# Premix and postmix of talking-heads attention on the four quarters of the array, two slots at a time

## Chip, core and metric

One NeuronCore of a Trainium2 chip runs the whole kernel. Its engines work side by side, each on its own queue in order: TensorE (PE, with its weight loads PEld), VectorE (DVE), ScalarE (ACT), GpSimd (POOL) and SyncE (SP), which here only issues transfers. SBUF and PSUM have 128 partitions; PSUM has eight banks of 2 KB a partition. The metric is the device time of one execution in microseconds (us).

## What is computed

All sizes are fixed: 4 batches, 12 heads, 448 positions, head size 64.

```
scores = q @ k.T / 8                             # per head: 448 x 448
scores = einsum('bhij,hg->bgij', scores, w_pre)  # premix over the heads
e      = exp(scores - max_j);  attn = e / (sum_j e + 1e-9)
attn   = einsum('bhij,hg->bgij', attn, w_post)   # postmix over the heads
x      = attn @ v                                # 1792 tokens x 768
g      = x @ w_in;  y = (g - tanh(g)) @ w_out    # hidden 2048
# then: soft routing of the tokens to 32 slots, 8 experts, and back
```

w_in and w_out come as 64-bit floats and are converted to 32 bits by integer operations during the attention.

## The kernel before

`talking_heads` takes the queries of a batch in chunks of 120, 120, 120 and 88, sixteen in all. `scores` (L266) makes sc for two heads at a time and ScalarE copies it to S (L274), queries on the partitions. A chunk is cut into slots of at most ten queries (`attention_chunks`), 12, 12, 12 and 9 slots, 180 in all. `regroup` (L291, SyncE) moves one slot from S to a tile D with (query, head) on 120 partitions and the 448 keys along the row.

One slot then goes through these steps. `premix` (L297): pm = wpre x D, one product with a 120 x 120 weight (w_pre repeated on the diagonal, built by `kron`), 448 columns, into one PSUM bank of tag "p" (two banks); VectorE takes the negative maximum mx of each row (L299). `expo` (L306, ScalarE): e = exp(pm + mx) and the row sums ss, read by a second small instruction. `guard` (L312, GpSimd) and `recip` (L318, VectorE): rv = 1 / (ss + 1e-9). `norm` (L323, GpSimd): wk = wpost x rv. `postmix` (L333): tm = e transposed x wk, four products, each with 112 keys of e as weight columns and the 120 columns of wk moving, into one bank of tag "t" (two banks); ScalarE copies tm to aT (L336). `values` (L357) multiplies aT by v when a chunk is complete: vx, two heads at a time on the two column halves of the array.

An fp32 product appears in the trace as two records on PE and two weight loads on PEld; transposes and the products of scores (fp32r) as one.

The main loop (L514) runs over the slots s. In step s it issues the regroup of slot s + 4, planned loads, premix(s), recip and norm of s - 1, the VectorE ends of earlier jobs, postmix(s - 3), expo(s) and guard(s), then scores of the next chunk (twelve products, their four copies spread over two steps), pieces of the weight conversion (f, fa, wi, wo), and at most two jobs: k and q transposes (kx, qx; L219, L245), values. A planner spreads these over the slots. The order in which the loop issues is the order on every engine. k and v lie with four consecutive keys on one partition, 112 partitions (JP); keys appear in that permuted order everywhere.

Of the kernel before, what the change touches and what calls it, by code (L numbers as in the profile page):

```python
# [19 lines left out]
JP = SEQ // NR  # L20
# [99 lines left out]
def attention_chunks():  # L120
    out = []
    for b in range(NB):
        for i0 in range(0, SEQ, CHUNK):
            n = min(CHUNK, SEQ - i0)
            w = -(-n // IB)
            out.append((b, i0, n, [(o, len(range(o, n, w))) for o in range(w)]))
    return out


def talking_heads(tc, ident, q, k, v, w_pre, w_post, xd, box, follow):  # L130
    nc = tc.nc
    R = IB * NH
# [5 lines left out]
    DB = 5  # L138
    T_LAG = 3
# [17 lines left out]

    def load_k(b, p):
        if b:
            t = er.tile([JP, NR, 2, HD], FP32, tag="kn", name="kn", bufs=NP)  # L160
            nc.sync.dma_start(out=t, in_=k[b, 2 * p:2 * p + 2].rearrange("e (p r) d -> p r e d", r=NR))
        else:
            t = er.tile([JP, 2, NR, HD], FP32, tag="kn", name="kn", bufs=NP)
            nc.sync.dma_start(out=t, in_=k[b, 2 * p:2 * p + 2].rearrange("e (p r) d -> p e r d", r=NR))
        nat_k[b, p] = t

    def load_v(b, hf):
        t = lt.tile([JP, NP, NR, HD], FP32, tag="vn", name="vn", bufs=3)
        nc.sync.dma_start(out=t, in_=v[b, hf * NP:(hf + 1) * NP].rearrange("h (p r) d -> p h r d", r=NR))
        nat_v[b, hf] = t  # L170
# [7 lines left out]
    def kron(name, w, scale, inner_g):  # L178
        rep = lt.tile([R, NH], FP32, tag=name + "r", name=name + "r", bufs=1)
        nc.scalar.dma_start(out=rep, in_=w.unsqueeze(0).to_broadcast([IB, NH, NH]))  # L180
        m = lt.tile([R, IB, NH] if inner_g else [R, NH, IB], FP32, tag=name, name=name, bufs=1)
        if inner_g:
            src = rep.unsqueeze(1).to_broadcast([R, IB, NH])
            pat = [[-NH, IB], [0, NH]]
            neg = [[NH, IB], [0, NH]]
        else:
            src = rep.unsqueeze(2).to_broadcast([R, NH, IB])
            pat = [[0, NH], [-NH, IB]]
            neg = [[0, NH], [NH, IB]]
        nc.gpsimd.tensor_scalar(out=m, in0=src, scalar1=scale, scalar2=None, op0=ALU.mult)  # L190
        nc.gpsimd.affine_select(
            out=m, in_=m, pattern=pat, compare_op=ALU.is_ge, fill=0.0, base=0, channel_multiplier=1)
        nc.gpsimd.affine_select(
            out=m, in_=m, pattern=neg, compare_op=ALU.is_ge, fill=0.0, base=NH - 1, channel_multiplier=-1)
# [19 lines left out]
    def k_pair(b, p):  # L214
        x, read = small_bank([128, NR, JP], "kx", None if b else "x")
        src = nat_k.pop((b, p))
        for r in range(NR):
            if b:
                nc.tensor.transpose(  # L219
                    out=x[:, r, :], in_=src[:, r].rearrange("p e d -> p (e d)"), identity=ident[:JP, :JP])  # L220
            else:
                for e in range(2):
                    nc.tensor.matmul(
                        x[64 * e:64 * e + 64, r, :], lhsT=src[:, e, r, :], rhs=ident[:JP, :JP], start=True, stop=True)
        x = x.rearrange("p r j -> p (r j)")
# [68 lines left out]
    def premix(s):
        n, o, m, r = rows(s)
        x = ps.tile([R, SEQ], FP32, tag="p", name="pm")
        nc.tensor.matmul(x[:r], lhsT=wpre[:r, :m, :], rhs=D_t.pop(s)[:r], start=True, stop=True)  # L297
        mx = lt.tile([R, 1], FP32, tag="mx", name="mx", bufs=3)
        nc.vector.tensor_reduce(out=mx[:r], in_=x[:r], op=ALU.max, axis=AX.X, negate=True)  # L299
        pp_t[s], mx_t[s] = x, mx  # L300

    def expo(s):
        n, o, m, r = rows(s)
        e = lt.tile([R, SEQ], FP32, tag="e", name="e", bufs=T_LAG + 1)
        ss = lt.tile([R, 1], FP32, tag="ss", name="ss", bufs=3)
        nc.scalar.activation(out=e[:r], in_=pp_t.pop(s)[:r], func=ACTF.Exp, bias=mx_t.pop(s)[:r], accum_out=ss[:r])  # L306
        e_t[s], ss_t[s] = e, ss

    def guard(s):
        n, o, m, r = rows(s)  # L310
        rv = lt.tile([R, 1], FP32, tag="rv", name="rv", bufs=3)
        nc.gpsimd.tensor_scalar(out=rv[:r], in0=ss_t.pop(s)[:r], scalar1=EPS, scalar2=None, op0=ALU.add)  # L312
        ss_t[s] = rv

    def recip(s):
        n, o, m, r = rows(s)
        rv = ss_t[s]
        nc.vector.reciprocal(out=rv[:r], in_=rv[:r])  # L318

    def norm(s):  # L320
        n, o, m, r = rows(s)
        wk = lt.tile([R, NH, IB], FP32, tag="wk", name="wk", bufs=T_LAG)
        nc.gpsimd.tensor_scalar(out=wk[:r], in0=wpost[:r], scalar1=ss_t.pop(s)[:r], scalar2=None, op0=ALU.mult)  # L323
        wk_t[s] = wk

    def postmix(s):
        n, o, m, r = rows(s)
        if o == 0:
            attn_t[n] = lt.tile([JP, NR, NH, CHUNK], FP32, tag="aT", name="aT", bufs=2)
        e, wk = e_t.pop(s), wk_t.pop(s)  # L330
        x = ps.tile([JP, NR, NH, IB], FP32, tag="t", name="tm", bufs=2)
# [1080 lines left out]
```

## Time and profile before

| | |
|---|---|
| median of 3 executions | 929.73 us (928.1 to 933.96) |
| profiled execution, span from first to last instruction | 926.1 us |
| TensorE busy | 894.8 us, 97% |
| VectorE, ScalarE, GpSimd busy | 564.2, 573.3, 295.6 us |
| DMA moved | 223.95 MB, 242 GB/s |
| chain of waits | PE 90%, DMA 4%, ACT 2%, DVE 2% |

The profile shows one execution. Busy time is the time in which an engine has at least one instruction running; matmuls overlap and their ends are modelled. The chain of waits follows the work that ended last back to the start, at each step to what released it. The shares of the whole span mix the attention with the products behind it, so the views that matter are those by stretches. The span is the profiled execution's own time as far as the profile shows it; the executions that were timed include what lies around it.

### The profile page before, as it was taken

The page shows a single profiled execution, that of the slowest core. Times are in us where ns is not written, and L with a number is a line of the kernel's source. Part 1 is how long each engine was busy: PE and PEld are TensorE (multiplying, and loading weights), DVE is VectorE, ACT ScalarE, POOL GpSimd, SP SyncE. Part 2 cuts the span into 40 slices and gives each one's busy share as a digit, 9 for nine tenths or more (in the row PEclk, how much of TensorE's full clock was granted, in tenths as well). Part 3 has the DMA queues.
Part 4 walks back from the last instruction along what each step waited for, and adds up shares of the span by engine and source line. Part 5 has one row for each costly group of instructions (what it writes and reads, how often), then busy time and mean ns, then how long its engine had stood idle before and what let it go on. Part 6 is the DMA issues. An engine that isn't in the chain of part 4 may idle for free.

```text
span 926.1 us, 19424 instructions
## 1 busy us (share of the span) xinstructions
PE 894.8 (97%) x6926; PEld 658.9 (71%) x6926; DVE 564.2 (61%) x1267; ACT 573.3 (62%) x1299; POOL 295.6 (32%) x499
## 2 busy tenths in 40 slices
PE   8989999999999999999999999999999998999995
PEld 6667777777777777777778677767776776875453
DVE  3566757767678676686555576566866677740103
ACT  4766767777777777777665667546664666730013
POOL 1464445644446544565431223000000014610000
PEclk9999999999999999999999999999999999998998
DMA  6988688866889766684457878669754536879998
GB/s 138 236 215 230 202 235 221 246 208 198 228 226 245 224 184 212 201 249 166 145 213 260 309 248 274 241 247 361 309 207 168 171 106 219 306 292 424 424 375 310
DMA packets 145780, 223.95 MB, mean 242 GB/s; under 512 B 60756, under 2 KB 127380, under 8 KB 142100
## 3 DMA queue, kind: packets, MB, share of 16 engines
q1 hardware_dynamic: 142336, 209.83, 70.6%
q10 hardware_dynamic: 3348, 12.87, 3.6%
q8 instruction: 56, 0.92, 0.4%
q14 instruction: 40, 0.33, 0.1%
HBM read 147.96 MB, written 36.18 MB: 199 GB/s over the span
## 4 chain that ended last, share of the span: by engine, by line
PE 90%; DMA 4%; ACT 2%; DVE 2%; issue 1%; POOL 0%; ACTq 0%; POOLq 0%; SPq 0%; DVEq 0%
PE hp L755 24%; PE pm L297 15%; PE tm L333 14%; PE vx L357 9%; PE sc L266 7%; DMA D<-S 3%; PE h L1197 3%; PE gt L826 3%; PE so L1238 2%; PE tz L1217 2%; PE lgp L876 2%; PE sp L958 1%; PE wt L845 1%; PE qx L245 1%; PE op L1294 1%
## 5 line engine op out<-in xcount | busy, mean ns | idle before, releaser
L333 PEld LDWEIGHTS tm<-wk,e 120*112 120x112 f32 (+1 forms) x1440 | 174.0, 177 | 70.6 <-issue 58.5
L299 DVE TENSOR_REDUCE mx<-pm 120x1 f32<-120x448 f32 x180 | 111.9, 622 | 126.0 <-PE pm L297 125.4
L336 ACT ACTIVATE aT<-tm 112x480 f32<-112x480 f32 x180 | 105.4, 585 | 120.1 <-PE tm L333 120.1
L297 PE MATMUL pm<-D,wpre 120*120 120x448 f32 x360 | 174.1, 566 | 5.2 <-DMA D<-S 4.7
L333 PE MATMUL tm<-wk,e 120*112 120x120 f32 (+1 forms) x1440 | 176.7, 266 | 1.0 <-POOL wk L323 1.0
L323 POOL TENSOR_SCALAR wk<-wpost,rv 120x120 f32<-120x120 f32 x180 | 124.8, 693 | 137.4 <-PE tm L333 116.0
L755 PE MATMUL hp<-xa,rg 128*128 128x512 f32 x576 | 152.5, 405 | 0.0
L755 PEld LDWEIGHTS hp<-xa,rg 128*128 128x128 f32 x576 | 102.5, 189 | 28.5 <-issue 10.7
L306 ACT ACTIVATE e<-pm,mx 120x448 f32<-120x448 f32 x180 | 113.4, 630 | 4.9 <-DVE rv L318 2.4
L717 POOL TENSOR_TENSOR rg<-rg 128x384 fp32r<-128x384 f32 x32 | 31.9, 1011 | 206.3 <-DVE rg L714 191.4
L274 ACT ACTIVATE S<-sc 120x448 f32<-120x448 f32 (+1 forms) x186 | 90.6, 543 | 7.3 <-PE sc L266 3.0
L357 PE MATMUL vx<-aT,vn 112*64 112x120 f32 (+1 forms) x1536 | 84.0, 263 | 0.0
L786 DVE SCALAR_TENSOR_TENSOR qd<-qd,sq 128x512 f32<-128x512 f32 (+1 forms) x62 | 38.3, 617 | 69.9 <-ACT mk L782 63.5
L357 PEld LDWEIGHTS vx<-aT,vn 112*64 112x64 f32 x1536 | 73.9, 137 | 6.1 <-issue 0.9
L775 ACT ACTIVATE sq<-hp 128x512 f32<-128x512 f32 (+1 forms) x62 | 32.8, 530 | 71.7 <-PE hp L755 71.7
L755 PE MATMUL hp<-xb,rg 128*128 128x512 f32 x288 | 74.8, 405 | 0.0
L312 POOL TENSOR_SCALAR rv<-ss 120x1 f32<-120x1 f32 x180 | 42.7, 237 | 97.0 <-ACT e L306 83.6
L297 PEld LDWEIGHTS pm<-D,wpre 120*120 120x120 f32 x360 | 51.4, 182 | 27.7 <-ACT e L306 10.7
L266 PE MATMUL sc<-khi,qT 64*120 64x448 f32 (+1 forms) x384 | 68.8, 387 | 0.8 <-DVE qT L249 0.8
L68 POOL TENSOR_TENSOR fa<-fa,f 128x384 f32<-128x384 f32 x64 | 65.2, 1019 | 5.3 <-issue 0.2
L755 PEld LDWEIGHTS hp<-xb,rg 128*128 128x128 f32 x288 | 52.0, 188 | 16.6 <-issue 6.3
L708 POOL TENSOR_TENSOR rg<-rg 128x768 fp32r<-128x768 f32 x13 | 24.0, 1845 | 67.8 <-PE gt L826 33.5
(177 smaller groups left out, 1351.6 us busy)
## 6 DMA issues: line engine op xcount, KB each, us to landing
ex<-in_moe_w_dram SPq DMA_DIRECT2D x25, 1536.0 KB
D<-S SPq DMA_DIRECT2D x172, 210.0 KB
rg<-wis SPq DMA_DIRECT2D x32, 768.0 KB
f<-in_moe_w_in_dram SPq DMA_DIRECT2D x32, 384.0 KB
f<-in_moe_w_out_dram SPq DMA_DIRECT2D x32, 384.0 KB
wis<-rg ACTq DMA_DIRECT2D x16, 768.0 KB
rg<-wi SPq DMA_DIRECT2D x26, 384.0 KB
wi<-fa SPq DMA_DIRECT2D x32, 192.0 KB
```

Source lines behind the costliest of these rows:

```text
L68: eng.tensor_tensor(out=out, in0=bits(a), in1=bits(p), op=ALU.add)
L266: nc.tensor.matmul(xs[e][0][:ni], lhsT=qT[n][s, l, p, :ni], rhs=kt[s], start=(i == 0), stop=(i == 2))
L274: nc.scalar.activation(out=dst, in_=xs[e][0][:ni], func=ACTF.Copy)
L297: nc.tensor.matmul(x[:r], lhsT=wpre[:r, :m, :], rhs=D_t.pop(s)[:r], start=True, stop=True)
L299: nc.vector.tensor_reduce(out=mx[:r], in_=x[:r], op=ALU.max, axis=AX.X, negate=True)
L306: nc.scalar.activation(out=e[:r], in_=pp_t.pop(s)[:r], func=ACTF.Exp, bias=mx_t.pop(s)[:r], accum_out=ss[:r])
L312: nc.gpsimd.tensor_scalar(out=rv[:r], in0=ss_t.pop(s)[:r], scalar1=EPS, scalar2=None, op0=ALU.add)
L323: nc.gpsimd.tensor_scalar(out=wk[:r], in0=wpost[:r], scalar1=ss_t.pop(s)[:r], scalar2=None, op0=ALU.mult)
L333: nc.tensor.matmul(x[:, c, :, :m], lhsT=e[:r, c * JP:(c + 1) * JP], rhs=wk[:r, :, :m], start=True, stop=True)
L336: nc.scalar.activation(out=attn_t[n][:, :, :, c0:c0 + m], in_=x[:, :, :, :m], func=ACTF.Copy)
L357: nc.tensor.matmul(x[64 * e:64 * e + 64, i, :ni], lhsT=nat_v[b, h // NP][:, h % NP, c, :], rhs=a[:, c, h, :ni], start=(c == 0), stop=(c == ...
L755: nc.tensor.matmul(hp, lhsT=r32(w[:, m, hl, cs]), rhs=r32(x_of(b, c, l)), start=(c == 0 and i == 0), stop=(c == KD - 1 and i == 2))
```

## The change

A slot's ten queries are split: queries 0 to 4 lie on partitions 4 to 63, queries 5 to 9 on 64 to 123, four zero rows ahead. The mixing of the heads never crosses queries, so the weight falls into two blocks of 64 x 64. Two slots (a pair) go together. Premix is four products of 64 x 64 with 448 columns: the row half is the half x of the queries, the column half is the slot i; the result xs[x] has the first slot on partitions 0 to 63 and the second on 64 to 127. Postmix is 32 products: for each x and each run c of 128 keys, slot i on row half i, key half z on column half z, 64 key columns of weight and 60 moving. To make this fit, keys lie on 128 partitions, four to a partition on the first 64 and three on the others, so k and v come in two transfers each. The slot count of a chunk is now even: 12, 12, 12, 10, 184 in all, 92 pairs. A pair takes both banks of "p" and, for postmix, both of "t". The copy to aT is a step of its own (`gather`), one loop step behind postmix; where a slot has fewer than ten queries it takes two instructions.

```diff
-    DB = 5
-    T_LAG = 3
+    DB = 6
+    T_LAG = 4
...
-            w = -(-n // IB)
+            w = 2 * -(-n // (2 * IB))
...
+    def load_rows(t, src):
+        nc.sync.dma_start(out=t[:64], in_=src[:, :JL].rearrange("h (p r) d -> p h r d", r=NR))
+        nc.sync.dma_start(out=t[64:, :, :NR - 1], in_=src[:, JL:].rearrange("h (p r) d -> p h r d", r=NR - 1))
...
     def regroup(s):
-        t = lt.tile([R, SEQ], FP32, tag="D", name="D", bufs=DB)
+        t = ds[s % DB]
-        nc.sync.dma_start(out=t[:r], in_=S_t[n][o:ni:w])
+        nc.sync.dma_start(out=t[4:4 + m * NH], in_=S_t[n][o:ni:w])
...
     def premix(s):
-        x = ps.tile([R, SEQ], FP32, tag="p", name="pm")
-        nc.tensor.matmul(x[:r], lhsT=wpre[:r, :m, :], rhs=D_t.pop(s)[:r], start=True, stop=True)
+        xs = [ps.tile([128, SEQ], FP32, tag="p", name="pm") for _ in range(2)]
+        d = [D_t.pop(s + i) for i in range(2)]
+        for x, k0, k1 in ((0, 0, 64), (1, 64, 64 + (m - IH) * NH)):
+            for i in range(2):
+                nc.tensor.matmul(
+                    xs[x][64 * i:64 * i + 64], lhsT=wpre[k0:k1], rhs=d[i][k0:k1], start=True, stop=True)
...
+            nc.vector.tensor_reduce(out=mx[:, x:x + 1], in_=xs[x], op=ALU.max, axis=AX.X, negate=True)
...
     def expo(s):
+            nc.scalar.activation(
+                out=es[x], in_=xs[x], func=ACTF.Exp, bias=mx[:, x:x + 1], accum_out=ss[:, x:x + 1])
...
     def norm(s):
+            wk = lt.tile([128, NH, IH], FP32, tag="wk", name="wk", bufs=2 * EB)
+            nc.gpsimd.tensor_scalar(out=wk, in0=wpost, scalar1=rv[:, x:x + 1], scalar2=None, op0=ALU.mult)
...
     def postmix(s):
-        for c in range(NR):
-            nc.tensor.matmul(
-                x[:, c, :, :m], lhsT=e[:r, c * JP:(c + 1) * JP], rhs=wk[:r, :, :m], start=True, stop=True)
+        xs = [ps.tile([128, 2, NR, NH, IH], FP32, tag="t", name="tm", bufs=2) for _ in range(2)]
+        for x in range(2):
+            for c in range(NR):
+                for i in range(2):
+                    for z in range(2):
+                        h = slice(64 * i, 64 * i + 64)
+                        j = min(128 * c + 64 * z, SEQ - 64)
+                        nc.tensor.matmul(
+                            xs[i][64 * z:64 * z + 64, x, c], lhsT=es[x][h, j:j + 64], rhs=wks[x][h],
+                            start=True, stop=True)
...
+        if s % 2 == 0:
+            if live:
+                premix(s)
+            for f in late:
+                f()
+            if 0 <= s - T_LAG < NS:
+                postmix(s - T_LAG)
+            if live:
+                expo(s)
+                guard(s)
+        else:
+            if s - 1 < NS:
+                recip(s - 1)
+                norm(s - 1)
+            for f in late:
+                f()
+            if 0 <= s - 1 - T_LAG < NS:
+                gather(s - 1 - T_LAG)
```

TensorE's queue in the middle of the attention, before (the number behind a name is the buffer; "x4" are four products in a row):

```order
L297 MATMUL pm_3951<-D_3794,wpre_134 120x448
L333 MATMUL tm_3960<-wk_3877,e_3839 112x120 x4
L297 MATMUL pm_3978<-D_3824,wpre_134 120x448
L333 MATMUL tm_3985<-wk_3909,e_3885 112x120 x4
L266 MATMUL sc_3997<-khi_2819,qT_3605 120x448
```

The same place after the change; the tm rows go on in this way, sixteen of them:

```order
L321 MATMUL pm_5043<-D_135,wpre_151 64x448
L321 MATMUL pm_5043<-D_136,wpre_151 64x448
L321 MATMUL pm_5044<-D_135,wpre_151 64x448
L321 MATMUL pm_5044<-D_136,wpre_151 64x448
L364 MATMUL tm_5052<-wk_4920,e_4898 64x60 x2
L364 MATMUL tm_5053<-wk_4920,e_4898 64x60 x2
L364 MATMUL tm_5052<-wk_4920,e_4898 64x60 x2
L364 MATMUL tm_5053<-wk_4920,e_4898 64x60 x2
```

Two slots' premix and postmix, which alternated, stand as one block of four and one of 32 products, and other products come only behind the block.

ScalarE's queue in the middle of the attention, before:

```order
L336 ACTIVATE aT_3779<-tm_3912 112x48x10
L306 ACTIVATE e_3918,ss_3919<-pm_3904,mx_3906 120x448
L47 ACTIVATE fa_3924<-f64_3681 128x384
L336 ACTIVATE aT_3779<-tm_3960 112x48x10
L306 ACTIVATE e_3966,ss_3967<-pm_3951,mx_3953 120x448
```

The same after:

```order
L333 ACTIVATE e_4898,ss_4900<-pm_4855,mx_4861 128x448
L333 ACTIVATE e_4899,ss_4900<-pm_4856,mx_4861 128x448
L295 ACTIVATE S_4461<-sc_4841 120x448
L295 ACTIVATE S_4461<-sc_4842 120x448
L267 ACTIVATE qT_4545<-qx_4911 128x360
L378 ACTIVATE aT_4830<-tm_4864 128x48x10
L378 ACTIVATE aT_4830<-tm_4865 128x48x10
L48 ACTIVATE fa_4927<-f64_4642 128x384
```

The copies of tm stood ahead of the e of the same step; they now stand behind the pair's two e and whatever the even step holds.

## Rows read from the trace of the kernel before

**Rows 1.** The page: span, busy time of the engines.

```profile
span 926.1 us, 19424 instructions
...
PE 894.8 (97%) x6926; PEld 658.9 (71%) x6926; DVE 564.2 (61%) x1267; ACT 573.3 (62%) x1299; POOL 295.6 (32%) x499
```

**Rows 2.** Busy time by stretches; columns in the first row.

```profile
core 0: us, PE busy (x) PEld busy (x) DVE busy (x) ACT busy (x) POOL busy (x), PEclk, DMA share, GB/s
...
22.00:60.00 38.00, 33.05 (x204) 22.99 (x205) 21.69 (x54) 28.75 (x74) 19.24 (x45) 1.00 0.90 228
...
150.00:200.00 50.00, 50.00 (x441) 38.19 (x440) 36.97 (x98) 38.01 (x95) 28.37 (x50) 1.00 0.90 249
...
250.00:300.00 50.00, 50.00 (x439) 38.19 (x438) 37.58 (x97) 37.54 (x93) 28.20 (x49) 1.00 0.91 239
```

**Rows 3.** The same view, 75 to 489 us.

```profile
75.00:489.00 414.00, 412.12 (x3623) 316.33 (x3623) 282.78 (x711) 300.35 (x741) 208.10 (x376) 1.00 0.73 213
```

**Rows 4.** The chain of waits, 75 to 489 us, shares by line.

```profile
by line: PE pm L297 32.1%; PE tm L333 31.3%; PE vx L357 17.7%; PE sc L266 12.9%; PE kx L219 1.7%; PE qx L245 1.7%; DMA D<-S 1.3%; PE hp L755 1.1%; issue 0.4%; DVE xa L741 0.3%; ACT e L306 0.2%; DVE mx L299 0.1%; POOL wk L323 0.1%; ACT S L27
```

**Rows 5.** The same stretch, premix's line alone (L297).

```profile
75.00:489.00 414.00, 151.89 (x314) 44.84 (x314) 1.00 0.73 213
```

**Rows 6.** The chain in order of time, 22 to 80 us: start, length, what.

```profile
37.50 10.50 DMA D<-S
...
66.69 1.79 PE vx L357 x32
...
69.72 5.53 DMA D<-S
```

**Rows 7.** TensorE in order of time (start, length, line, operation), plain slots, then scores.

```profile
254.94 1.01 PE L297 MATMUL pm<-D,wpre 120*120 120x448 f32 x2
255.79 0.98 PE L333 MATMUL tm<-wk,e 120*112 120x120 f32 x8
256.61 0.92 PE L297 MATMUL pm<-D,wpre 120*120 120x448 f32 x2
...
258.54 0.37 PE L266 MATMUL sc<-klo,qT 64*120 64x448 f32 x2
258.74 0.57 PE L266 MATMUL sc<-khi,qT 64*120 64x448 f32 x4
```

**Rows 8.** The same, windows 854.985 to 855.013 and 855.44 to 855.48 us: four strips.

```profile
854.99 0.13 PEld L1197 LDWEIGHTS h<-ex,siT 128*32 128x32 f32 x4
854.99 0.64 PE L1197 MATMUL h<-ex,siT 128*32 128x512 f32 x4
...
854.99 1.07 PE L1197 MATMUL h<-ex,siT 128*32 128x512 f32 x8
```

**Rows 9.** Weight loads of vx, windows 302.00 to 302.02 and 302.05 to 302.07 us.

```profile
302.00 0.14 PEld L357 LDWEIGHTS vx<-aT,vn 112*64 112x64 f32 x2
...
302.00 0.20 PEld L357 LDWEIGHTS vx<-aT,vn 112*64 112x64 f32 x4
```

**Rows 10.** Weight loads of 128 columns, 521 us.

```profile
520.99 0.97 PEld L865 LDWEIGHTS wq<-seld,ex 96*128 96x128 f32 x8 [0.25 <-ACT ex L860]
```

**Rows 11.** The page's groups: busy, mean ns, idle time before.

```profile
L299 DVE TENSOR_REDUCE mx<-pm 120x1 f32<-120x448 f32 x180 | 111.9, 622 | 126.0 <-PE pm L297 125.4
...
L323 POOL TENSOR_SCALAR wk<-wpost,rv 120x120 f32<-120x120 f32 x180 | 124.8, 693 | 137.4 <-PE tm L333 116.0
```

**Rows 12.** ScalarE in order of time, 307 to 310 us.

```profile
307.24 0.59 ACT L336 ACTIVATE aT<-tm 112x480 f32<-112x480 f32 x1 [0.39 <-PE tm L333]
307.71 0.62 ACT L306 ACTIVATE e<-pm,mx 120x448 f32<-120x448 f32 x1
...
308.31 0.96 ACT L274 ACTIVATE S<-sc 88x448 f32<-88x448 f32 x2
309.16 0.55 ACT L47 ACTIVATE fa<-f 128x384 f32<-128x384 f32 x1
```

**Rows 13.** SyncE's issues at the start.

```profile
18.82 6.02 SPq L291 DMA_DIRECT2D D<-S  x7
```

More of the change, by code (lines that the diff above doesn't have):

```diff
@@ new lines, in kron @@
+        if pre:
+            m = lt.tile([128, 64], FP32, tag=name, name=name, bufs=1)
+            nc.gpsimd.memset(m, 0.0)
+            for x in range(2):
+                nc.gpsimd.tensor_copy(
+                    out=m[64 * x:64 * x + 64, 4:], in_=big[64 * x:64 * x + 64, IH * x:IH * x + IH].rearrange("p i g -> p (i g)"))
+        else:
+            m = lt.tile([128, NH, IH], FP32, tag=name, name=name, bufs=1)
+            for x in range(2):
+                nc.gpsimd.tensor_copy(out=m[64 * x:64 * x + 64], in_=big[64 * x:64 * x + 64, x])
@@ L296, in premix @@
[L296 to L307 removed]
+        m = rows(s)[2]
@@ L309, in guard @@
+        pp_t[s], mx_t[s] = xs, mx
+    def expo(s):
+        es = [lt.tile([128, SEQ], FP32, tag="e", name="e", bufs=2 * EB) for _ in range(2)]
+        ss = lt.tile([128, 2], FP32, tag="ss", name="ss", bufs=2)
+        xs, mx = pp_t.pop(s), mx_t.pop(s)
+        for x in range(2):
+            nc.scalar.activation(
+                out=es[x], in_=xs[x], func=ACTF.Exp, bias=mx[:, x:x + 1], accum_out=ss[:, x:x + 1])
+        e_t[s], ss_t[s] = es, ss
     def guard(s):
-        n, o, m, r = rows(s)
@@ L311, in guard @@
[L311 to L312 removed]
+        rv = lt.tile([128, 2], FP32, tag="rv", name="rv", bufs=2)
+        nc.gpsimd.tensor_scalar(out=rv, in0=ss_t.pop(s), scalar1=EPS, scalar2=None, op0=ALU.add)
         ss_t[s] = rv
     def recip(s):
[L316 to L318 removed]
+        nc.vector.reciprocal(out=ss_t[s], in_=ss_t[s])
@@ L320, in norm @@
     def norm(s):
[L321 to L324, printed above, removed]
-    def postmix(s):
[L327 to L331, printed above, removed]
-        for c in range(NR):
-            nc.tensor.matmul(
-                x[:, c, :, :m], lhsT=e[:r, c * JP:(c + 1) * JP], rhs=wk[:r, :, :m], start=True, stop=True)
-        c0 = sum(z for q, z in chunks[n][3] if q < o)
-        nc.scalar.activation(out=attn_t[n][:, :, :, c0:c0 + m], in_=x[:, :, :, :m], func=ACTF.Copy)
+        rv = ss_t.pop(s)
@@ new lines, in gather @@
+    def gather(s):
+        for i, x in enumerate(tm_t.pop(s)):
+            n, o, m = rows(s + i)
+            if o == 0:
+                attn_t[n] = lt.tile([128, NR, NH, CHUNK], FP32, tag="aT", name="aT", bufs=2)
+            c0 = sum(z for q, z in chunks[n][3] if q < o)
+            out = attn_t[n].rearrange("p r h i -> p (r h) i")
+            x = x.rearrange("p x r h i -> p (r h) x i")
+            if m == 2 * IH:
+                nc.scalar.activation(
+                    out=out[:, :, c0:c0 + m].rearrange("p a (x i) -> p a x i", x=2), in_=x, func=ACTF.Copy)
+            else:
+                nc.scalar.activation(out=out[:, :, c0:c0 + IH], in_=x[:, :, 0], func=ACTF.Copy)
+                nc.scalar.activation(out=out[:, :, c0 + IH:c0 + m], in_=x[:, :, 1, :m - IH], func=ACTF.Copy)
@@ L513, in talking_heads @@
     s = 0
-    while s < NS + T_LAG + 2 or jobs or late:
+    while s < NS + T_LAG + 3 or jobs or late:
         live = s < NS
```

96 lines of the change are left out of this document (53 added, 43 removed).

## Prediction

> **What bounds the kernel now.** I read the page first, then a table by stretches, then the chain of waits of the long stretch, then single instructions. The profiled execution has a span of 926.1 us [rows 1]; the three times shown have a median of 929.73 us, 3.6 us more, and the sum below is made against 926.1. TensorE is busy 97% of the span, but that is an average over two halves. The slot loop runs from 22 to 489 us; everything behind it is untouched by the change.
>
> From 75 to 489 us TensorE is busy 412.12 of 414 us; ScalarE 300.35, VectorE 282.78, GpSimd 208.10, the DMA engines 0.73 [rows 3]. The chain of waits there is pm 32.1%, tm 31.3%, vx 17.7%, sc 12.9%: TensorE waits for nothing [rows 4]. pm has 314 records, two to an fp32 product, so this is 157 slots, 78.5 pairs of 5.27 us [rows 5].
>
> From 22 to 75 us it is another story. TensorE is busy 33.05 of 38 us (87%) while the DMA engines are at 0.90 [rows 2], and the chain holds transfers D<-S, of 10.50 and 5.53 us among them [rows 6]: premix waits for its rows. A faster premix gains nothing there.
>
> **The change, part by part.**
>
> *Premix.* A plain slot shows what it costs: pm starts at 254.94, tm at 255.79, the next pm at 256.61 [rows 7]. The last gap, 0.82 us, is tm's; the pm behind it (0.92 us with its drain) costs 0.75 until tm may follow, so pm + tm are 1.57 us a slot and 3.14 us a pair. After, a pair has four 64x64 products of the same 448 columns, eight records on four quarters. If the quarters run together, that is two rounds of 0.375 us, 0.75, and I put 0.05 for the first weights: 0.80 us a pair in place of 1.50. The trace has no 64x64 product. It has the two halves of the idea apart. Halves of the rows: sc, 448 columns in one pass (0.19 us, half of a pm record's two passes), comes in pairs 0.20 us apart, at 258.54 and 258.74 [rows 7]. Parts of the columns: four h records on four strips take 0.64 us together and eight take 1.07 [rows 8], so a further round of four costs 0.43 us, the streaming time of one (512 columns where pm's 448 take 0.375). Bounds: 0.75 when both compose, 1.50 when only one does.
>
> *Postmix.* Before, 16 records a pair of 120 columns, 0.82 us a slot [rows 7]. After, 32 products, 64 records of 64 weight columns and 60 moving columns, 16 rounds on four quarters. Two things can set a round. The moving part is half of tm's 0.10 us: 0.05 us. The weight load: two vx loads of 64 columns, one on each column half, end together after 0.14 us, four after 0.20 [rows 9], so a second load on the same half costs 0.06 us; eight of 128 columns take 0.97 us [rows 10], 0.12 each, 0.06 for 64. Loads of the two halves run together. So a round is 0.06 us, bound by the loads, and a pair costs 16 x 0.06 = 0.96, with the first load 0.98 us in place of 1.64. Bounds: 0.82 (the moving part alone) and 64 x 0.055 = 3.5 us (every load by itself). I take 0.98, since it is the load that the vx rows show on halves.
>
> How fast records can follow one another matters at 64 a pair. In a window of 0.028 us four loads and four products of h have all begun [rows 8], so records of different strips go out some 0.007 us apart with their loads. A round of four has 0.06 us to go out in. [...]
>
> *TensorE's sum.* 5.27 - 3.34 us (pm and tm by their 63.4% of the chain) leaves 1.93 us a pair for vx, sc, kx, qx; none of these changes its columns. The queries of the 88-row chunks now make 10 slots in place of 9, so 184 slots, 161 of them behind the first 23: 80.5 pairs. TensorE then needs 0.80 + 0.98 + 1.88 = 3.66 us a pair, 295 us.
>
> *What is late next.* With TensorE that short, the others have no slack. ScalarE: 300.35 us / 80.5 = 3.73 us a pair; the 88-row chunks' slots copy aT in two pieces (40 slots; a second piece between nothing and 0.55 us, the fa row of 384 elements [rows 12]; I take 0.2), 0.1 more. VectorE 3.5. The DMA engines 0.73 x 414 / 80.5 = 3.75 us. All lie between 3.5 and 3.85, so the loop no longer has one bound but four.
>
> The pair also loses double buffering: pm's two banks and tm's two banks now both belong to one pair. So the next postmix waits for both aT copies, and these stand behind two e on ScalarE, which wait for mx, which waits for pm. Followed round for two pairs: tm 0.98, other products 1.88, pm 0.80 and its drain 0.17, the first mx 0.62 [rows 11] with 0.1 of handing over, two e at 0.60 (307.71 to 308.31 [rows 12]), on average one S copy 0.43 and 0.3 of fa and qT, two aT at 0.47: 7.4 us, 3.7 a pair. Queued behind the waiting e are the S copies that free the banks of sc; behind the waiting tm stand sc and vx.
>
> Four demands of 3.5 to 3.85 us that must meet in one order will not fill each other's gaps. The one stretch where TensorE shares the bound is 22 to 60 us: 87% busy. 3.66 / 0.87 = 4.2 us a pair. Bounds: 3.7 (no friction) and 4.7 (as much friction again).
>
> *DMA.* Bytes and rows stay; k and v tiles come as two transfers instead of one, 32 more issues on SyncE, 0.86 us each by the D<-S rows (seven in 6.02 us [rows 13]): 28 us over the loop, before which SyncE's 180 D<-S issues are 155 us of 467; it has room. In 150 to 200 and 250 to 300 us the DMA share is 0.90 and 0.91 already [rows 2]: these cannot go below 45 us each, while 4.2/5.27 would make them 40. I add 2 x 5 us.
>
> *At the start.* The six first kn loads become twelve. At the 0.86 us of an issue that is up to 5 us if all of it is on the path, nothing if the warm-up products cover it; I take 2. The new GpSimd setup (zero rows, larger masks) lies ahead of the first pm at 21.9 us, on an engine that is nearly idle until then. Its 22 operations at wk's 0.69 us [rows 11] would be 15 us; what went over 21.9 would cost its full length.
>
> *GpSimd and VectorE in the loop.* rv and its reciprocal halve in number, wk stays two a pair at half the columns: nothing on the path, since GpSimd has 208 of 414 us.
>
> **Sum.** 22 to 75 us: unchanged. 75 to 489: 80.5 x 4.2 = 338, and 10 for the DMA: 348 in place of 414, -66. Start +2. 926.1 - 64 = 862, and 3.6 outside the span: **866 us**.
>
> **Rivals.**
> 1. *TensorE stays the only bound.* ScalarE and DMA times are unions that include waits and contention, and shrink when pressed. Then 3.66 us a pair, 295, and 10 for the DMA: -109 + 2, **823 us**. For it: two demands of 0.73 left TensorE no gap at all before. Against: single banks, and the 87% of 22 to 60 us. 0.10.
> 2. *Postmix gains little: records go out too slowly, or two quarters run at a time.* tm stays at 1.6 to 1.86 us a pair (32 rounds of 0.058), TensorE needs 4.28 to 4.54; it is then the longest demand again, and half the friction (a factor of 1.075) makes 4.6 to 4.9 us a pair, 370 to 394, with no DMA addition: **888 to 912 us**. If premix runs in twos as well (pm 1.5), TensorE needs 5.24 us, 422: **940 us** at most, about no change. For it: no row has 64 records in a microsecond. Against: the h rows. 0.14, and 0.06 for about no change. [...]
> 3. *The other side: weight loads of the quarters go one after another.* tm 64 x 0.055 = 3.5 us, 0.80 + 3.5 + 1.88 = 6.2 us a pair on TensorE alone; over 92 pairs 570 us in place of 467: **1,035 us**. The change turns into a loss when a pair exceeds 414 / 80.5 = 5.14 us; without friction that is tm at 2.46 us, 38 ns a record, with half of it 2.1 us, 33 ns. vx, with two halves, makes a record per 56 ns (32 in 1.79 us [rows 6]). Against: vx is bound by its 120 columns, not by loads, and its loads overlap. 0.11.
>
> **How the numbers follow.** The likeliest, 0.59: 866, its own range 840 to 895 (3.9 to 4.55 us a pair). Rival 1 0.10, rival 2 0.14, about no change 0.06, rival 3 0.11. The range 820 to 920 leaves out some 0.03 below and 0.17 above. A measurement of this kernel can tell about 1%, 9 us, from no change: faster 0.83, same 0.06, slower 0.11.
>
> **What would show it.** tm: 64 records in about 1.0 us, rounds 0.06 us apart; pm: the pair's four products within 0.8 us and a drain. In 75 to 475 us TensorE below 90% busy, ScalarE and DMA each near 0.9. Chain: pm and tm together under 45%, with ACT e, ACT aT or DMA D<-S in it. TensorE at 97% with a shorter loop would be rival 1; tm records 25 ns or more apart rival 2; 50 ns rival 3. [...]

## Result and the profile after

| | before | after |
|---|---|---|
| median of the executions run together | 928.99 us (4) | 918.12 us (4; 913.11 to 922.78) |
| ratio to before, 95% interval | | 0.9874, 0.9825 to 0.9923 |
| profiled execution, span | 926.1 us | 921.1 us |

The change made the kernel 1.3% faster; 866 us had been forecast, 7% faster. Repeated later on another occasion, the changed kernel took 918.96 us (0.9881, 0.9848 to 0.9913). Its four executions lie within 1.1% of each other, those of the kernel before within 0.6%. A ratio is taken over executions in the fast state, less than 1.5% above the fastest of their kernel; this leaves out two of the four executions of the run with f on ScalarE's queue and one of ten of the run with a second xs.

The page of the changed kernel, answering to [rows 1], with its queues (packets, MB, share of 16 engines):

```profile
span 921.1 us, 28684 instructions
...
PE 841.1 (91%) x11750; PEld 599.0 (65%) x11750; DVE 559.1 (61%) x1183; ACT 574.2 (62%) x1351; POOL 250.6 (27%) x431
...
q1 hardware_dynamic: 143808, 209.84, 73.4%
...
q8 instruction: 93, 1.52, 0.7%
```

The same two queues of the kernel before:

```profile
q1 hardware_dynamic: 142336, 209.83, 70.6%
...
q8 instruction: 56, 0.92, 0.4%
```

The same 209.8 MB take 0.734 x 921.1 = 676 us of the 16 engines in place of 0.706 x 926.1 = 654: there are 1,472 packets more, and the mean packet takes 75.2 ns in place of 73.5. TensorE has 4,824 products' and as many loads' records more, and its instruction packets (16 KB each) went from 56 to 93.

Busy time by stretches of the changed kernel, answering to [rows 2] and [rows 3]:

```profile
core 0: us, PE busy (x) PEld busy (x) DVE busy (x) ACT busy (x) POOL busy (x), PEclk, DMA share, GB/s
75.00:489.00 414.00, 372.11 (x8207) 269.90 (x8204) 291.52 (x664) 313.59 (x820) 169.66 (x313) 0.97 0.81 223
22.00:60.00 38.00, 29.91 (x433) 17.57 (x433) 16.38 (x37) 24.60 (x61) 8.97 (x25) 0.94 0.80 181
150.00:200.00 50.00, 43.38 (x1008) 30.39 (x1004) 35.22 (x83) 36.04 (x96) 21.49 (x38) 0.98 0.90 229
250.00:300.00 50.00, 44.65 (x984) 31.94 (x983) 36.85 (x88) 39.47 (x111) 23.34 (x40) 0.97 0.88 235
```

TensorE is no longer full, as forecast; but the loop is hardly shorter. The first pm begins at 29.33 us (21.87 before), the last tm ends at 484.8 (488.8 before): 455.4 us for 92 pairs, 4.95 us each. Behind the loop nothing changed: 436.3 us to the end of the span, 437.3 before.

The chain of waits from 75 to 489 us, answering to [rows 4], and its longest pieces (start, length, what):

```profile
by line: DMA D<-S 13.6%; PE vx L403 10.4%; PE pm L321 10.3%; PE tm L364 8.8%; ACT e L333 8.2%; PE sc L287 7.7%; DVE mx L325 6.9%; issue 6.3%; ACT S L295 3.6%; PE hp L813 2.1%; PE kx L241 2.1%; DMA rg<-wi 2.1%; ACT aT L378 1.9%; DVE fa L58 1
...
179.81 8.27 DMA D<-S
188.82 9.21 DMA D<-S
272.74 7.64 DMA D<-S
296.19 17.48 DMA D<-S x2
```

pm and tm, 63.4% before, are 19.1%; nothing has taken their place alone. TensorE in order of time, two plain pairs, answering to [rows 7]:

```profile
219.79 0.98 PE L321 MATMUL pm<-D,wpre 64*64 64x448 f32 x8
220.59 1.11 PE L364 MATMUL tm<-wk,e 64*64 64x60 f32 x64
221.63 0.44 PE L287 MATMUL sc<-khi,qT 64*88 64x448 f32 x2
...
223.41 0.98 PE L321 MATMUL pm<-D,wpre 64*64 64x448 f32 x8
224.21 1.11 PE L364 MATMUL tm<-wk,e 64*64 64x60 f32 x64
```

From start to next start, pm takes 220.59 - 219.79 = 0.80 us and tm 221.63 - 220.59 = 1.04 us a pair; 0.80 and 0.98 had been forecast. These two pairs stand 3.62 us apart. The quarters do what they should.

A ledger of TensorE from first pm to last tm, worked out from its single records (each counted from the end of the one before it) shows where the gain went:

| us | before | after |
|---|---|---|
| pm | 154.2 | 110.7 |
| tm | 147.6 | 104.5 |
| sc | 61.9 | 76.1 |
| vx | 76.7 | 81.3 |
| kx and qx | 15.4 | 25.5 |
| hp, issued early | 4.3 | 4.3 |
| idle | 6.8 | 53.0 |

pm and tm gave 87 us. Idle time took 46 of them, and the others' records 29: kx and qx by some 10 (a kx of four products, 448 columns in all before and after, went from 0.39 to 0.68 us; why is not shown), sc by 14, most of it at the full clock too (a record takes 138 ns in place of 117, as products start late without leaving TensorE idle: above, the pairs at 221.63 and 221.91 us begin 0.28 us apart, those of [rows 7] 0.20), and vx by 5, most of it the clock: 41 us of the loop were granted a clock of 0.50, which cost some 20 (an estimate: work at half the pace, since the 32 products of vx take 1.86 us at a clock of 1.00 and took 3.47 at 146.22 us, at 0.50). At 0.80 and 1.04 us the 92 pairs would need 74 us for pm and 96 for tm. The 111 and 105 of the ledger also hold what the lower clock cost, and premix blocks that stretched: in 19 of them the third weight load waited for the second slot's D while two records ran alone.

### The profile page after: what moved, and what is told of

It reads as the page before. It is cut to its first block, busy times and chain, and to the rows that moved or that the text cites. A ratio compares the mean times of both kernels' runs of the same rounds, so it can differ in the third digit from the quotient of the medians.

```text
span 921.1 us, 28684 instructions
## 1 busy us (share of the span) xinstructions
PE 841.1 (91%) x11750; PEld 599.0 (65%) x11750; DVE 559.1 (61%) x1183; ACT 574.2 (62%) x1351; POOL 250.6 (27%) x431
## 3 DMA queue, kind: packets, MB, share of 16 engines
q1 hardware_dynamic: 143808, 209.84, 73.4%
## 4 chain that ended last, share of the span: by engine, by line
PE 64%; DMA 12%; ACT 9%; DVE 8%; issue 4%; POOL 1%; SPq 1%; ACTq 0%; POOLq 0%; DVEq 0%
PE hp L813 24%; DMA D<-S 8%; PE pm L321 6%; PE vx L403 5%; PE tm L364 5%; PE sc L287 4%; ACT e L333 4%; DVE mx L325 3%; PE h L1255 3%; PE gt L884 3%; PE so L1296 2%; PE tz L1275 2%; ACT S L295 2%; DMA rg<-wi 2%; PE lgp L934 2%
## 5 line engine op out<-in xcount | busy, mean ns | idle before, releaser
L333 ACT ACTIVATE e<-pm,mx 128x448 f32<-128x448 f32 x184 | 115.2, 632 | 94.6 <-DVE mx L325 92.4
L364 PEld LDWEIGHTS tm<-wk,e 64*64 64x64 f32 x5888 | 120.3, 139 | 65.8 <-issue 40.5
L325 DVE TENSOR_REDUCE mx<-pm 128x1 f32<-128x448 f32 x184 | 105.9, 616 | 83.8 <-PE pm L321 83.8
L364 PE MATMUL tm<-wk,e 64*64 64x60 f32 x5888 | 128.7, 225 | 18.8 <-issue 9.5
L321 PE MATMUL pm<-D,wpre 64*64 64x448 f32 (+2 forms) x736 | 116.3, 579 | 25.0 <-DMA D<-S 19.6
L350 POOL TENSOR_SCALAR wk<-wpost,rv 128x60 f32<-128x60 f32 x184 | 89.6, 510 | 16.0 <-DVE rv L343 13.5
L403 PE MATMUL vx<-aT,vn 128*64 128x120 f32 (+1 forms) x1536 | 88.1, 269 | 0.8 <-issue 0.8
L403 PEld LDWEIGHTS vx<-aT,vn 128*64 128x64 f32 x1536 | 77.8, 141 | 6.9 <-issue 3.4
L378 ACT ACTIVATE aT<-tm 128x480 f32<-128x480 f32 x144 | 75.9, 593 | 0.1
L287 PEld LDWEIGHTS sc<-khi,qT 64*120 64x120 f32 (+1 forms) x384 | 46.9, 182 | 22.7 <-issue 5.4
```

The source lines that it names most:

```text
L287: nc.tensor.matmul(xs[e][0][:ni], lhsT=qT[n][s, l, p, :ni], rhs=kt[s], start=(i == 0), stop=(i == 2))
L321: nc.tensor.matmul(xs[x][64 * i:64 * i + 64], lhsT=wpre[k0:k1], rhs=d[i][k0:k1], start=True, stop=True)
L325: nc.vector.tensor_reduce(out=mx[:, x:x + 1], in_=xs[x], op=ALU.max, axis=AX.X, negate=True)
L333: nc.scalar.activation(out=es[x], in_=xs[x], func=ACTF.Exp, bias=mx[:, x:x + 1], accum_out=ss[:, x:x + 1])
L350: nc.gpsimd.tensor_scalar(out=wk, in0=wpost, scalar1=rv[:, x:x + 1], scalar2=None, op0=ALU.mult)
L364: nc.tensor.matmul(xs[i][64 * z:64 * z + 64, x, c], lhsT=es[x][h, j:j + 64], rhs=wks[x][h], start=True, stop=True)
```

## Experiments

Each ratio is to the kernel before, run beside it. The texts name the theories by letters: that the transfers hold the loop up (A in the first texts, T later), that the order and the round on the engines do (B, K, R), SyncE's queue (Q), or TensorE's instruction packets (I).

**D fetched further ahead.** D_AHEAD 4 to 6, DB 6 to 8:

```diff
-    D_AHEAD = 4
-    DB = 6
+    D_AHEAD = 6
+    DB = 8
```

> The changed kernel with eight buffers for D instead of six and each regroup issued six slots ahead instead of four (the job windows of q move with it). Nothing else differs. Theory A, that premix waits because D<-S comes late behind other transfers: two more slots ahead are some 9 us more, more than the extra latency seen, so the waits of pm on DMA D<-S (44.7 us on the weight loads in the changed kernel) fall below 15 us and the time by 20 to 40 us, to 880 to 898. Theory B, that the pair's single pairs of PSUM banks and the order on ScalarE set the pace: D was early enough in most pairs, the waits only move to ACT e and ACT aT, and the time stays within 6 us of 918.

Measured 926.66 us, 0.9962 (0.9931 to 0.9992): no gain, rather a loss of 8 us against the changed kernel. The waits of premix's products for D, 75 to 400 us, of the changed kernel and of this one (us in total, times, longest):

```profile
PE pm L321 <- DMA D<-S: 12.9, 15, 2.4
PE tm L364 <- issue: 8.6, 6, 2.7
PE sc L287 <- DVE xs L413: 4.4, 10, 0.5
```

```profile
PE sc L287 <- DVE xs L413: 16.3, 12, 4.7
PE kx L241 <- ACT S L295: 6.4, 7, 3.4
...
PE pm L321 <- DMA D<-S: 0.4, 1, 0.4
```

The wait for D is gone and has come back at other places. So D's lead is not the cause. On top of it, a second buffer for the tile whose store then led the chain:

```diff
-            xs_t[n] = lt.tile([128, NP, CHUNK], FP32, tag="xs", name="xs", bufs=1)
+            xs_t[n] = lt.tile([128, NP, CHUNK], FP32, tag="xs", name="xs", bufs=2)
```

> D is fetched six slots ahead instead of four, into eight buffers instead of six (as in the earlier run that did this alone, 926.7 us), and the tile from which the attention output is stored gets a second buffer, since in that run the store of it was the largest single wait of the chain (13.7% between 75 and 420 us). Theory K (the lead of single transfers and the buffers behind them hold the loop up; once D and this store no longer do, the gain shows): 885 to 905 us. Theory T (the transfers as a whole are the bound, and a wait taken away from one comes back at another): 913 to 927 us.

928.08 us, 0.997 (0.9939 to 1.0001): no gain either. Theory K falls.

**f loads left out.** Behind the first five, the f loads are not issued and their tiles are used again:

```diff
+        if len(self.raw) == self.bufs:
+            r = self.raw[self.n % self.bufs]
+            self.n += 1
+            self.t[j] = [r]
+            return
```

> The changed kernel without 59 of the 64 loads of 64-bit weights (f), 23 MB of the transfers in the slot loop; the conversion then works on what lies in the five tiles, so its output is not the reference's. All instructions of the engines stay. Theory A (transfers): D<-S, k and v and TensorE's own instructions come faster, the loop loses 30 to 45 us, the time is 875 to 890, and waits of tm for nothing that the profile shows (2.67 us at 144.8 us) go. Theory B (banks and order): less than 12 us, 906 or more.

Measured 881.43 us, 0.9488 (0.9462 to 0.9513). With every other load left out:

```diff
+        if self.n > self.bufs and self.n % 2:
+            self.t[j] = [r]
+            return
```

> The changed kernel with every other f load left out (behind the first five), output not the reference's. All 59 left out took 72 us of DMA time and 37 us of kernel time. Theory T (the loop is as long as the transfers need): half the dose, half the effect, 896 to 904 us. If only the fullest stretches hold the loop up, most of the 37 us is back already, 880 to 890 us.

895.62 us, 0.9638 (0.9606 to 0.9669). And the control, the same loads left out of the kernel before:

> The control for the run that left 59 of 64 f loads out of the changed kernel (881.4 us, 37 us less): the same loads left out of the kernel before, so that its output is not the reference's either (the f tiles of the first five pieces are converted again and again). Theory T (only a loop with less work on TensorE is held up by the 16 DMA engines): TensorE idles 6.8 us in this kernel's loop, so at most 8 us are to be had, 921 to 929 us. If instead the transfers cost either kernel about the same, it gains some 30 us, 890 to 900 us, and the run on the changed kernel says nothing about this change.

924.6 us, 0.9959 (0.9935 to 0.9983). The loads cost the kernel before 4 us and the changed one 37, some 22 of them for the first half. The first row is the kernel before, 75 to 400 us, then the control, the changed kernel, half the loads and none (columns as in [rows 2]):

```profile
75.00:400.00 325.00, 324.15 (x2836) 248.09 (x2837) 228.62 (x577) 241.62 (x598) 165.82 (x298) 1.00 0.77 219
```

```profile
75.00:400.00 325.00, 325.00 (x2856) 248.57 (x2852) 228.70 (x580) 240.25 (x596) 166.34 (x298) 1.00 0.53 156
```

```profile
75.00:400.00 325.00, 291.71 (x6337) 209.88 (x6337) 233.55 (x536) 248.31 (x652) 137.65 (x249) 0.97 0.86 227
```

```profile
75.00:400.00 325.00, 305.07 (x6997) 219.42 (x6989) 255.19 (x591) 269.70 (x710) 150.22 (x271) 0.99 0.78 214
```

```profile
75.00:400.00 325.00, 310.36 (x7250) 223.83 (x7245) 262.57 (x609) 279.67 (x735) 157.28 (x284) 1.00 0.64 185
```

In the changed kernel TensorE's busy time and its records per stretch rise as the DMA share falls (0.86, 0.78, 0.64); in the kernel before 0.77 or 0.53 makes no difference.

**Bytes or queue.** Leaving loads out also takes issues from SyncE, behind which D stands. Two runs part these. In the first, every f load is issued with an eighth of its bytes:

```diff
+            z = self.CV if full else self.CV // 8
```

> The changed kernel with every f load still issued, in its place and with its waits, but behind the first five only an eighth of its bytes (48 KB instead of 384); output not the reference's. Leaving the loads out altogether gave 881.4 us, and took away both their bytes and 59 issues of SyncE's queue, each of which can hold up the D issues behind it while it waits for a free buffer. Theory T (bytes on the 16 DMA engines): most of the 37 us comes back with the bytes, 882 to 890 us. Theory Q (SyncE's queue: D is issued late because it stands behind f): nothing comes back, 912 to 922 us.

In the second, ScalarE issues the whole loads:

```diff
-            self.nc.sync.dma_start(
+            self.nc.scalar.dma_start(
```

> The changed kernel with all f loads whole, but issued by ScalarE's queue instead of SyncE's, so that no D stands behind them on SyncE. Theory T: the same bytes on the same engines, 913 to 925 us. Theory Q: D is issued earlier and the 37 us of the run without these loads come back in good part, 885 to 900 us. ScalarE, which has 574 us of 921 busy, pays for 64 issues; at the 0.5 us that such an issue takes on SyncE that is 32 us over the loop, which may show as a loss of up to some 10 us under either theory.

Measured 885.36 us (0.9542, 0.952 to 0.9565) and, with ScalarE issuing, 911.58 and 916.28 us (0.9854, 0.982 to 0.9889; the median of all four is 921.0). From 75 to 400 us, in this order:

```profile
75.00:400.00 325.00, 307.74 (x7166) 222.15 (x7162) 261.25 (x604) 276.66 (x728) 156.20 (x281) 1.00 0.68 191
```

```profile
75.00:400.00 325.00, 295.33 (x6602) 211.88 (x6596) 241.31 (x555) 254.80 (x670) 141.50 (x254) 0.97 0.87 232
```

It is the bytes: 33 us come back with them, though the packets are as many as before (143,808), and with the queue no more than the scatter.

**Premix without the maximum.** e without mx, bias 0, so that the round premix, mx, e, premix is 0.7 us shorter, with all bytes and with the thin loads:

```diff
-                out=es[x], in_=xs[x], func=ACTF.Exp, bias=mx[:, x:x + 1], accum_out=ss[:, x:x + 1])
+                out=es[x], in_=xs[x], func=ACTF.Exp, bias=zero, accum_out=ss[:, x:x + 1])
```

> The changed kernel without the two mx of a pair: the exponent is taken without subtracting the row's maximum (bias 0), so the output may differ from the reference's. In the trace of the changed kernel e follows the first mx by 0.1 us and the mx of a pair take 1.16 us of VectorE, so the round premix, mx, e, next premix gets 0.7 us shorter of some 3.6, and VectorE 1.2 us of some 3.5 a pair. Theory R (the round through the one pair of premix banks holds the loop): a pair gets 0.4 to 0.7 us shorter, 855 to 882 us. Theory T (with all bytes to move the DMA engines hold it): 905 to 920 us.

> The same on top of the run with thin f loads (885.4 us, an eighth of the bytes behind the first five loads), output not the reference's. There the DMA engines have room (0.68 from 75 to 400 us), and a pair still takes 4.5 us where TensorE's products need 3.7. Theory R: the round is what is left, so a pair gets 0.4 to 0.7 us shorter, 822 to 850 us. If something else holds the loop there (the order of the products on TensorE), 878 to 887 us.

Measured 915.61 us (0.9833, 0.9785 to 0.9882) and 860.2 us (0.9274, 0.9197 to 0.9352). All four, by medians (of separate occasions) and by the length of a pair from first pm to last tm:

| | all bytes | thin f loads |
|---|---|---|
| with mx | 918.1 us, pair 4.95 | 885.4 us, pair 4.56 |
| without mx | 915.6 us, pair 4.89 | 860.2 us, pair 4.29 |

The shorter round is worth 3 us, no more than the scatter, while all bytes are to be moved, and 25 us once they are not. So there are two limits one behind the other: the transfers, then what mx belongs to, the round or VectorE's work. The chain of the run with both, 75 to 400 us, is TensorE's again:

```profile
by line: PE tm L370 18.2%; PE pm L330 18.0%; PE vx L409 18.0%; PE sc L296 13.3%; DMA D<-S 7.6%; ACT e L339 6.4%; ACT S L304 3.5%; PE kx L250 2.8%; DMA xa<-xd 2.7%; ACT aT L384 2.6%; issue 2.5%; DMA xd<-xs 2.0%; PE qx L275 1.7%; DMA wi<-fa 0
```

The run takes away more than mx's place in the round, since VectorE also has 1.2 us less to do a pair; which of the two counts was not parted.

**Wider weights in postmix.** Where a block of 128 keys is whole, one product of 128 columns on each row half in place of two of 64:

```diff
+                        nc.tensor.matmul(
+                            xs[i][:, x, c], lhsT=es[x][h, 128 * c:128 * c + 128], rhs=wks[x][h], start=True, stop=True)
```

> Postmix takes weights of 64 rows and 128 columns where a whole block of 128 keys is there, so a pair has 20 products instead of 32, two at a time instead of four. TensorE's program gets shorter by 12 products x 2 passes x (load and product) x 92 pairs = 4,416 instructions; by the packets of the traces so far (93 instead of 56 for 9,650 more instructions) that is 17 instruction packets of 16 KB fewer. Theory I (TensorE's instructions come late on full DMA engines: the waits called issue and the half clock behind them, some 8 us of stall and 13.6 us at half clock in the loop): the waits called issue halve, 905 to 912 us. Theory T (the transfers as a whole are the bound): nothing changes, 913 to 923 us. Both hold only if the block of products stays near 0.93 us; if a load of 128 columns takes as long as the old 120x112 one (8 records in 0.82 us), the block takes up to 2 us and the time rises, to 950 us or more.

Measured 944.19 us, 1.0169 (1.0136 to 1.0203). TensorE in order of time, one postmix and what follows:

```profile
221.68 0.88 PE L363 MATMUL tm<-wk,e 64*128 64x60 f32 x12
222.49 0.34 PE L367 MATMUL tm<-wk,e 64*64 64x60 f32 x8
222.76 0.88 PE L363 MATMUL tm<-wk,e 64*128 64x60 f32 x12
223.57 0.34 PE L367 MATMUL tm<-wk,e 64*64 64x60 f32 x8
223.84 0.43 PE L287 MATMUL sc<-khi,qT 64*88 64x448 f32 x2
```

The block takes 223.84 - 221.68 = 2.16 us in place of 1.04: the column half is worth a factor of two in postmix. That fits the weight loads as its bound (0.12 us for 128 columns [rows 10]), but fewer products at a time would look the same, and the run does not part them. From 75 to 400 us:

```profile
75.00:400.00 325.00, 323.97 (x4652) 234.20 (x4652) 229.35 (x522) 243.28 (x634) 132.92 (x239) 1.00 0.82 221
```

TensorE is busy 323.97 of 325 us at a DMA share of 0.82, and the kernel is slower than before: with TensorE the longer, these transfers left it 1.03 us of gaps. The instruction packets fell to 76, but with TensorE the bound the run cannot tell what these cost in the changed kernel.

**What did not help.** Larger packets for k:

```diff
-            t = er.tile([128, NR, 2, HD], FP32, tag="kn", name="kn", bufs=NP)
+            t = er.tile([128, 2, NR, HD], FP32, tag="kn", name="kn", bufs=NP)
+            load_rows(t, src)
```

> The k tiles of the batches after the first are loaded in the layout of the first, so that their packets are 768 or 1,024 bytes instead of 256; k is then turned by 8 products of half the width for each pair of heads instead of 4. 16,128 packets of 256 bytes (24 ns each in the changed kernel) become 4,032 (64 ns): 24.2 us less 16.1 us on 16 engines, so the DMA time of the loop falls from 376 to about 368 us. Theory T (the loop is as long as the transfers need, as leaving out 72 us of DMA time gave back 37 us): 4 to 8 us faster, 908 to 915 us. Theories I and K: no change or 1 us slower from the added products, 915 to 923 us. The scatter of this kernel, near 1%, makes the difference hard to see in the time; the DMA share and the time of the loop's DMA packets in the trace tell whether the edit did what it should.

916.16 us, 0.9862 (0.9833 to 0.9891). The queue took 0.729 x 913.2 = 666 us in place of 676, and the time fell by 2 to 3 us, within the scatter. On top of it, f pieces later with eight products more in the warm-up, and then a planner that looks at pairs as well:

```diff
-        due = 6 + i * (NS - D_AHEAD - 17) // len(pieces)
+        due = 12 + int((NS - D_AHEAD - 23) * (i / len(pieces)) ** 0.8)
...
+        if p == 1:
+            for _ in range(8):
+                nc.tensor.matmul(warm, lhsT=ident, rhs=ident, start=True, stop=True)
```

> The kernel with the larger k packets (916.2 us), and two edits more. The f pieces begin six slots later and lie denser towards the end of the attention, since the DMA engines were busy 0.85 to 0.91 of the time from 75 to 350 us and 0.57 to 0.79 behind that. Eight products of the warm-up are put into the wait behind the second k tile at 9 us, behind which TensorE ran at half clock from 10.6 to 17.4 us. Theory T: the same transfers in a more even row give back 5 to 8 us, and the start 2 us, as the first premix comes at 25 to 26 us instead of 27.6: 905 to 911 us. Without it only the start shows: 912 to 917 us.

```diff
-        return min(range(lo, hi + 1), key=lambda s: (load[kind][s], s))
+        return min(range(lo, hi + 1), key=lambda s: (load[kind][s] + load[kind][s ^ 1], s))
```

> As the run beside it, and the planner looks at both slots of a pair when it seeks a quiet place for qx, vx and the pieces of the conversion, since the change issues in pairs and some pairs held kx, qx and vx at once (6.05 us of TensorE work instead of 4.54). Theory K (single long pairs hold up the loop behind them): 5 to 10 us less than the run beside it. Theory T: within 4 us of it.

920.13 us (0.9899, 0.9869 to 0.9929) and 928.78 us (0.9992, 0.9961 to 1.0023). Neither helped; the second lost 9 us against the run beside it, which neither theory had foreseen. In the first of them the DMA share from 75 to 400 us fell to 0.81 and TensorE was busy no longer (290.10 us), against what the runs with fewer bytes show at 0.78; how the transfers bunch must count beside their sum, and these runs do not say how. The first pm came at 25.12 us, but at 24.63 without the warm-up products too. Two early runs: the second halves of the first k tiles on ScalarE's queue, and the copy to aT right behind e, in the even step:

```diff
-            load_rows(t, src)
+            load_rows(t, src, nc.scalar)
```

> The changed kernel with the second half of each of the first six k tiles issued on ScalarE's queue instead of SyncE's. Before the change the first pm began at 21.87 us, after it at 29.33. If the doubled issues on SyncE are what holds the first transposes up and lets the granted clock fall to 0.5 from 11 to 21 us, the first pm comes back to 22 to 24 us and the time falls by 5 to 7 us, to 911 to 913. If it is the amount of data or the different shapes, it stays at 918.

```diff
+            if 0 <= s - T_LAG < NS:
+                gather(s - T_LAG)
...
-            if 0 <= s - 1 - T_LAG < NS:
-                gather(s - 1 - T_LAG)
```

> The changed kernel with the copies of tm to aT (gather) one step earlier on ScalarE, right behind the pair's two e, ahead of the score copies, fa and q copies of the even step. Theory B (the next postmix waits for these copies because a pair holds both tm banks): the loop of tm, other products, pm, mx, e, copies gets shorter by 0.4 to 0.7 us for two pairs, 15 to 30 us over the kernel, 888 to 903. Theory A (transfers) and a third theory, that pairs with kx, qx and vx at once are the long ones: no more than 5 us either way, and the score copies come later, which may cost as much.

928.07 us (0.9978, 0.9939 to 1.0017; first pm at 33.37) and 932.07 us (1.0034, 1.0006 to 1.0061). Both are slower than the changed kernel, so neither the issues on SyncE nor the late copies are shown to hold it up. And the changed kernel as it is, once more:

> The changed kernel once more, unchanged, on the same chip as the three runs that go with it: its first four times lay between 913 and 923 us, so 918 us within 5 is expected by every theory, and the others of this call are read against it.

918.96 us, as said above.

## Why the prediction was wrong

*Premix and postmix: right for a plain pair.* 0.80 and 1.04 us where 0.80 and 0.98 had been put. Rivals 2 and 3 fall: 64 records in 1.04 us are 16 ns each. No run shows the 1.6 us a pair of rival 2, nor the 25 ns a record that go with it; the two plain pairs above took 1.04 us. Rival 1 falls too, as TensorE was idle for 53 us of the loop. The choice of the vx rows [rows 9] for the weight loads was good.

*The others' 1.88 us: nearly right.* pm, tm, and the others at their old length with the longer kx and qx come to 0.80 + 1.04 + 1.83 = 3.67 us a pair; 3.66 had been put. By these lengths TensorE would do the loop in 92 x 3.67 = 338 us. It took 455.4. What lies beside the work was misjudged (idle time, stretched blocks, the lower clock): 117 us, 1.28 a pair, where 4.2 - 3.66 = 0.54 and the 10 us for the DMA had been allowed.

*The step that failed: "3.66 / 0.87 = 4.2 us a pair", with the DMA engines counted as one of four demands at 3.75 us, and only two stretches, 10 us, as bound by them.* Both terms were too small. Without the 10 us the forecast loop is 53 + 338 = 391 us. With thin f loads it took 419.5: the friction was put 28 us too low. With all bytes it took 455.4: the bytes add 36 us by these two traces (33 by the medians) where 10 had been allowed. The split is not a clean one, since the thin run still has other transfers to wait for. Of the 36, some 14 come by way of the clock (an estimate from its rows: 41 us of the loop at the lower level in place of 13.7).

The demand itself was too small: 0.73 x 414 us were divided by the pairs, but the packets of the new loop take 377 us, 4.1 a pair. Packets did take longer in the runs with the fuller engines (those of 1,792 bytes, 75 to 400 us, on average 97.8 ns at a share of 0.86, 93.1 with half the f loads at 0.78, 88.9 with none at 0.64). That does not explain the rise: in the run with wider weights, whose loop is longer than the one before, they took 0.714 x 941.1 = 672 us too. Where it comes from stays open. A pair of 4.2 us would have needed 4.1 / 4.2 = 0.98 of the engines all through the loop; of the changed kernel's 50 us stretches from 100 to 450 us none is over 0.90.

That is no ceiling. Around the start of the loop the share was higher, and behind it, with packets of 1,536 and 12,288 bytes, it passes 1 (it adds the packets' times, which can overlap), here in the changed kernel:

```profile
30.00:80.00 50.00, 38.94 (x681) 25.15 (x682) 23.07 (x53) 31.47 (x82) 15.51 (x41) 0.86 0.94 209
850.00:900.00 50.00, 48.05 (x550) 24.47 (x548) 4.94 (x15) 6.82 (x13) 1.44 (x5) 1.00 1.03 399
```

And half of the f loads, at a share of 0.78, still cost 14 us beside none. So transfers cost this loop time by degrees, long before the engines were full; the prediction let them count only where the share stood at 0.90 already [rows 2].

*The 87% of 22 to 60 us [rows 2] was the wrong row for friction.* That stretch was itself held by transfers [rows 6], so the number was a DMA limit taken for a mixture of four. The round, put at 3.7 us a pair if followed for two pairs, is the second limit: with thin loads a pair takes 4.56, without mx 4.29. Friction with most f bytes gone is then 4.56 - 3.67 = 0.9 us, not 0.54. That it was the premix banks' round is supported by the run without mx, not parted from VectorE's load.

*The start: a miss of size.* +2 us had been put for the doubled kn issues, up to 5 as a bound; the first pm came 7.5 us later (5.7 in the repeat). SyncE's last kn issue ends at 9.99 us in place of 6.34; and TensorE, after its wait of 2.02 us at 9.3, ran the second kx at a granted clock of 0.50, which held for 10.2 us from 11.25 us:

```profile
8.16 1.14 PE L245 MATMUL kx<-ident,kn 128*64 128x128 f32 x16 [0.48 <-DMA kn<-in_k_dram]
11.32 1.96 PE L245 MATMUL kx<-ident,kn 128*64 128x128 f32 x16 [2.02 <-DVE klo L253]
```

1.96 us where the same sixteen records took 1.14. In the five runs whose clock held until the first pm, this came at 24.6 to 26.3 us; with 3.4 us at the lower level at 26.3 and 26.4, with 10.2 at 29.33. So the new start costs some 3 to 4 us without the clock (24.6 to 26.3 against 21.87), and the rest comes with it. That the issues on SyncE are the cause is not shown: with half of them on ScalarE's queue the last on SyncE ended at 7.73 us, and the first pm came at 33.37.

*What was named and came:* DMA D<-S in the chain (13.6%), where premix waited for D (12.9 us from 75 to 400 us). The clock of 0.50 in the loop (41 us, some 20 lost) is in no term of the forecast. ScalarE near 0.9, named as a sign, did not come: 313.59 of 414 us. The run with D further ahead shows that the wait for D is where the lack of transfers surfaces, not its cause.

In sum, 52 us were missed. The start is 5.5 of them; the loop, 455.4 us in place of 53 + 348 = 401, is 54, of which 28 are the friction and 26 the transfers; 1 comes back behind it, and 6.6 since the profiled execution stands 3 us above its median, not 3.6 below. The repeat's loop took 449.2 us, so these parts are good to some 6 us. The run without mx gives back 25 of the friction's 28. That 918 us lies within the widest range stated, 820 to 920, is chance: its upper end was drawn for rival 2, whose slow records did not come.

## What to carry to other kernels

When an edit shortens the engine that bounds a loop, work out the share that the DMA engines would then need, and doubt a forecast that asks for nearly all of them: here the forecast pair asked for 0.98, and transfers cost time at 0.78 already. Transfers that cost 4 us under a full TensorE cost 37 once it had gaps, and a wait that was taken away came back at another buffer (with D further ahead, pm's waits for D fell from 12.9 to 0.4 us, and those of sc for xs rose from 4.4 to 16.3); taking away bytes, not single waits, tells this in one run. Take the friction of a mixture only from a stretch of which one knows what held it up.

## What was not expected of the hardware

TensorE waited in the middle of a postmix, for nothing that the program waits for. In order of time, changed kernel:

```profile
141.28 0.86 PE L364 MATMUL tm<-wk,e 64*64 64x60 f32 x43
144.80 0.70 PE L364 MATMUL tm<-wk,e 64*64 64x60 f32 x17 [2.67 <-issue]
```

A 16 KB instruction packet began at 142.4 us, inside this wait and 7.9 us after the one before it, and took 1.02 us; TensorE went on 1.4 us after its end. From 144.4 us, 6.8 us ran at a granted clock of 0.50:

```profile
144.40:151.20 6.80, 6.40 (x64) 4.68 (x67) 1.00 (x2) 1.91 (x7) 1.44 (x3) 0.50 0.76 185
```

Four such waits of 1.5 to 2.7 us stand between 75 and 400 us of this trace; without the f loads, with the same 93 packets, the longest is 0.29 us. 37 packets more for TensorE's 9,648 records more are 261 records a packet. That the late packet makes the wait is inferred from these times and was not tried by itself: the run with fewer packets had another bound.
